# Attention beside moe 1: exponentials go by a transfer into tiles of float32r words and are transposed from there

## The chip, the cores and the metric
The kernel runs on one core of one Trainium2 chip. The metric is the device time of one execution in microseconds (us). TensorE does the matmuls, VectorE, ScalarE and GpSimd the elementwise work (DVE, ACT and POOL in the profile), and 16 DMA engines move data, issued by SyncE (SP), GpSimd or ScalarE.

## The reference
Three steps follow each other, all in float32:

```
attention  q, k, v of 4 x 12 heads x 448 x 64:  q and k normed by rms over 64 and scaled by g_q, g_k
           softmax(q k^T / 8) v  -> x of 1792 tokens x 768
moe 1      sigmoid(x w_gate) * (x w_val), then @ w_out      (768 -> 1536 -> 768)
moe 2      8 experts, each token goes to the one with the largest logit:
           relu(x w1[e]) @ w2[e]  (768 -> 1024 -> 768), times its softmax weight and its output gate
```

## The kernel before, in words
Attention works on 24 pairs of heads. A pair has 8 slots; a slot is 112 queries of one head against all 448 keys, so there are 192 slots (`NSLOT`), numbered n. In `attn_slot(n)` stand: the scores of slot n+1 (two float32r matmuls of 448 columns into PSUM tile `s`), `soft_max(n)` (VectorE multiplies by the inverse norms of the keys and takes the row maximum, `e<-s,rb`, L377 and L380; ScalarE takes the exponential in place and its row sum, L381), `transp(n-2)` (four TensorE transposes of 112 x 112 against `ident` into PSUM tile `t`, L410, evicted to `et` by ScalarE at L418, or by VectorE in one slot of eight, L416), and, once in four slots, `av`, the matmuls of the transposed exponentials with v (L431).

Moe 1 is done in two halves of 896 tokens. Its first half is interleaved with the second half of attention: from slot 101 on, the main loop calls moe steps and attention slots in turn by a table of costs (3.4 for an `up`, 1.0 for a `down`), and between slots 96 and 101 the first weights are fetched. Every moe product takes three matmuls, since x and the weights are split into a high and a low float32r word (`xh`, `xl`, `whi`, `wlo`); `up` is at L555, `down` at L578. The weights of the first half come as 64-bit words: SyncE fetches a piece of 384 KB into `w` (L93), ScalarE and VectorE make float32 of it (L99 to L106), which goes to a buffer in DRAM (`wf`) for the second half of moe 1, and ScalarE and GpSimd or VectorE split it (L121, L123). `lead_turn`, `lead_mul` and `lead_put` (L510 to L540) fold the router's weights into w_out. From 60% of the steps on, rows of zeros are written to the gather table `xg` (L814, L815).

The order in each engine's queue is set by a scheduler that goes by its own estimates of cost; each engine then works its queue in order. Buffers come from pools: `lot("e", 4, 4)` gives the exponentials four buffers, and four more until slot 88 (`l[2] = None`), after which the extra pools are closed and those of moe 1 opened at slot 96. Each instruction waits by semaphores for its operands and its buffer. Moe 2 (from about 960 us) gathers tokens by expert into float32r tiles by DMA and transposes these against a float32r identity (`identr`, L940).

Of the kernel before, what the change touches and what calls it, by code (L numbers as in the profile page):

```python
# [8 lines left out]
F32 = mybir.dt.float32  # L9
F32R = mybir.dt.float32r  # L10
# [7 lines left out]
B, H, S, D = 4, 12, 448, 64  # L18
NT, DM, DFF, NE, FF = 1792, 768, 1536, 8, 1024
CH = 112  # L20
# [14 lines left out]
PARTS = 2  # L35
# [9 lines left out]
def attn_moe_moe_kernel(ctx, tc, qk, tokqk, tokv, g, wup, wout, wr, w1, w2, out):  # L45
    nc = tc.nc
# [3 lines left out]
    const = ctx.enter_context(tc.tile_pool(name="const", bufs=1))  # L50
# [8 lines left out]
    wf = dram.tile([3 * NF, 128, WO], F32, name="wf")  # L59

    ident = const.tile([128, 128], F32, name="ident")
    gg = const.tile([128, 1], F32, name="gg")
    tri = const.tile([128, 128], BF16, name="tri")
    ones = const.tile([128, 128], BF16, name="ones")
# [109 lines left out]
    def lot(name, bufs, more, space=None):  # L174
        kw = {} if space is None else dict(space=space)
        lots[name] = [moe1.enter_context(tc.tile_pool(name=name, bufs=bufs, **kw)), bufs, None, more, {}, kw]
# [6 lines left out]
    def tile_of(name, shape, dtype, tag):  # L183
        pool, bufs, pool2, more, turns, _ = lots[name]
        i = turns.get(tag, 0)
        turns[tag] = i + 1
        if pool2 is not None and i % (bufs + more) >= bufs:
            pool = pool2
        return pool.tile(shape, dtype, tag=tag, name=tag)
# [6 lines left out]
    lot("sw", 1, 0)  # L196
    lot("rs", 1, 1)
    lot("rb", 2, 1)
    lot("e", 4, 4)
    lot("sm", 6, 6)  # L200
    lot("et", 4, 4)
    lot("xr", 1, 2)
# [5 lines left out]
    mp = {}  # L208

    def open_moe():  # L210
        for name, bufs in (("acc", 1), ("h", 3), ("t", 2), ("w64", PARTS), ("wt", 1)):
            mp[name] = moe1.enter_context(tc.tile_pool(name=name, bufs=bufs))
        mp["m"] = moe1.enter_context(tc.tile_pool(name="ps_m", bufs=3, space=PSUM))
        mp["acc_t"] = mp["acc"].tile([128, NBLK, WO], F32, name="acc")
# [82 lines left out]
    def row_bank():  # L297

        if lots["ps_k"][2] is not None:
            return lots["ps_k"][2].tile([128, 4, CH], F32, tag="k", name="k")  # L300
        return tile_of("ps_t", [128, 4, CH], F32, "t")
# [47 lines left out]

    order = [(0, 0), (0, 1), (1, 0), (1, 1), (0, 2), (0, 3), (1, 2), (1, 3)]  # L350
    NSLOT = 8 * NPAIR
    s_t, e_t, et_t, av_t, rs_t = {}, {}, {}, {}, {}
    sum_t = [const.tile([CH, 8, 2], F32, name=f"sum{i}") for i in range(3)]
    for t in sum_t:
# [2 lines left out]
    def scores(n):  # L357
        if not 0 <= n < NSLOT:
            return
        p = n // 8  # L360
        h, c = order[n % 8]
        ps = tile_of("ps_s", [CH, S], F32, "s")
        lhs = Q_t[p][:, h, c * CH:(c + 1) * CH]
        nc.tensor.matmul(ps, lhsT=lhs, rhs=K1_t[p][:, h, :], start=True, stop=False)  # L364
        nc.tensor.matmul(ps, lhsT=lhs, rhs=K2_t[p][:, h, :], start=False, stop=True)  # L365
        s_t[n] = ps

    def soft_max(n):
        if not 0 <= n < NSLOT:
            return  # L370
        p = n // 8
        h, c = order[n % 8]
        ps = s_t.pop(n)
        e = tile_of("e", [128, S], F32, "e")[0:CH]
        m = tile_of("sm", [CH, 2], F32, "m")
        i = h * 4 + c
        nc.vector.tensor_tensor_reduce(  # L377
            out=e, in0=ps, in1=rb_t[p][:, h, :], scale=r_t[p][:, i:i + 1], scalar=-3.0e38, op0=ALU.mult, op1=ALU.max,
            accum_out=m[:, 0:1])
        nc.vector.tensor_reduce(out=m[:, 1:2], in_=m[:, 0:1], axis=AX.X, op=ALU.max, negate=True)  # L380
        nc.scalar.activation(  # L381
            out=e, in_=e, func=ACTF.Exp, scale=1.0, bias=m[:, 1:2], accum_out=sum_t[p % 3][:, i, 0:1])
        e_t[n] = e

    def sums(p):
        sm = tile_of("sm", [CH, 8], F32, "sum")

        nc.vector.tensor_reduce(out=sm, in_=sum_t[p % 3], axis=AX.X, op=ALU.add)
        nc.vector.reciprocal(out=sm, in_=sm)
        ps = row_bank()  # L390
        nc.tensor.transpose(ps[0:8, 0, :], sm, ident[0:CH, 0:CH])
        rr = tile_of("rs", [8, CH], F32, "rr")
        nc.vector.tensor_copy(out=rr, in_=ps[0:8, 0, :])
        nc.sync.dma_start(out=rsd[p], in_=rr)
        t = tile_of("rs", [128, S], F32, "rs")
        for h in range(2):
            nc.sync.dma_start(
                out=t[64 * h:64 * h + 64],
                in_=rsd[p:p + 1, 4 * h:4 * h + 4].rearrange("o c q -> o (c q)").to_broadcast([64, S]))
        rs_t[p] = t  # L400

    def transp(n):
        if not 0 <= n < NSLOT:
            return
        p = n // 8
        h, c = order[n % 8]
        e = e_t.pop(n)
        ps = tile_of("ps_t", [128, 4, CH], F32, "t")
        for kc in range(4):
            nc.tensor.transpose(ps[0:CH, kc, :], e[:, kc * CH:(kc + 1) * CH], ident[0:CH, 0:CH])  # L410
        if c % 2 == 0:
            et_t[p, h, c // 2] = tile_of("et", [CH, 4, 2 * CH], F32, "et")
        et = et_t[p, h, c // 2]
        dst = et[:, :, (c % 2) * CH:(c % 2 + 1) * CH]
        if n % 8 == 2:
            nc.vector.tensor_copy(out=dst, in_=ps[0:CH])  # L416
        else:
            nc.scalar.activation(out=dst, in_=ps[0:CH], func=ACTF.Copy)  # L418

    def av(n):  # L420
        if not 0 <= n < NSLOT or n % 4 != 3:
            return
        p = n // 8
        hf = (n % 8) // 4
        if hf == 0:
            av_t[p] = tile_of("ps_a", [128, S], F32, "a")
        ps = av_t[p]
        ets = [et_t.pop((p, h, hf)) for h in range(2)]
        for kc in range(4):
            for h in range(2):  # L430
                nc.tensor.matmul(  # L431
                    ps[64 * h:64 * h + 64, hf * 2 * CH:(hf + 1) * 2 * CH], lhsT=v_t[p][:, h, kc, :],
                    rhs=ets[h][:, kc, :], start=(kc == 0), stop=(kc == 3))

    def features(p):
        b, pr = divmod(p, H // 2)
        t = tile_of("xr", [128, S], F32, "xr")
        nc.vector.tensor_tensor(out=t, in0=av_t.pop(p), in1=rs_t.pop(p), op=ALU.mult)
        if b < 2:
            hi = x_p.tile([128, S], F32R, tag=f"xh{b}_{pr}", name="xh")  # L440
            lo = x_p.tile([128, S], F32R, tag=f"xl{b}_{pr}", name="xl")
            nc.gpsimd.tensor_copy(out=hi, in_=t)
            nc.gpsimd.tensor_tensor(out=lo, in0=t, in1=hi, op=ALU.subtract)
            xh[b, pr], xl[b, pr] = hi, lo
        else:
            nc.sync.dma_start(out=xs[b - 2, pr], in_=t)
# [33 lines left out]
    def attn_slot(n):  # L480
        p, i = divmod(n, 8)
        scores(n + 1)
        soft_max(n)
        transp(n - 2)
        if i == 0 and n > 0:
            sums(p - 1)
        av(n - 3)
        if i == 4 and n > 8:
            features(p - 1)
        la = 2 if p < NPAIR // 2 - 3 else 1  # L490
        if p == 0:
            prep(i)
        if p > 0 and i == 0:
            splits(p + la)
        if p > 0 and i == 1:
            stats(min(2 * p + 4, p + 6))
            krows(p + la)
        if i == 4:
            load_v(p + 1)
# [272 lines left out]

    def setup():
        make_identity(nc, ident)
        warm = const.tile([128, 1], F32, name="warm")
        nc.vector.memset(warm, 0.0)
        nc.scalar.activation(out=warm, in_=warm, func=ACTF.Exp)
        gt = const.tile([128, 2], F32, name="gt")
        nc.sync.dma_start(out=gt, in_=g)
        attn_loads0()  # L780
        nc.vector.tensor_tensor(out=gg, in0=gt[:, 0:1], in1=gt[:, 1:2], op=ALU.mult)
        nc.vector.tensor_scalar(out=gg, in0=gg, scalar1=float(D) ** -0.5, scalar2=None, op0=ALU.mult)
# [52 lines left out]
    n = 0  # L835
# [4 lines left out]
    n = 1  # L840
    while n < NSLOT // 2 + 5:
        attn_slot(n)
        n += 1
        if n == NSLOT // 2 - 8:
            for l in lots.values():
# [24 lines left out]

    for tg in range(2):
        for k in range(KD):
            t = tile_of("e", [128, S], F32, "e")
            nc.sync.dma_start(out=t, in_=xs[tg, k])
            hi = x_p.tile([128, S], F32R, tag=f"xh{tg}_{k}", name="xh")
            lo = x_p.tile([128, S], F32R, tag=f"xl{tg}_{k}", name="xl")
            nc.scalar.activation(out=hi, in_=t, func=ACTF.Copy)
            (nc.gpsimd if k >= 3 else nc.vector).tensor_tensor(out=lo, in0=t, in1=hi, op=ALU.subtract)
            xh[tg, k], xl[tg, k] = hi, lo
# [308 lines left out]
```

## Time and profile before

| | |
|---|---|
| median of 3 runs | 1289.23 us (1287.64 to 1289.48) |
| profiled execution | 1288.62 us, span of its instructions 1286.8 us |
| TensorE busy | 1185.8 us, 92% of the span, mean granted clock 0.966 |
| VectorE, ScalarE, GpSimd busy | 722.1, 577.1, 382.4 us |
| moved by DMA | 191.92 MB, 149 GB/s on average |

The page gives the span in 40 slices of 32 us; attention alone fills the first six, attention beside moe 1 the next fourteen, the rest of moe 1 goes to about slice 30, and moe 2 is the end. A matmul's duration is from its start to a modelled end, and matmuls are pipelined: what one costs in a stream is the distance to the next one's start. "Idle" before an instruction is the time its engine stood, and the arrow names what released it.

### The profile page before, as it was taken

Reading aid. Unit: us, or ns where it says so; the run is one execution under the profiler, and the core shown is the slowest. Engines: PE = TensorE matmul, PEld = TensorE weight load, DVE = VectorE, ACT = ScalarE, POOL = GpSimd, SP = SyncE. Lnnn points to the kernel's source line nnn. Section 1 sums busy time; section 2 is a strip of 40 time slices with the busy share of each in tenths; the row PEclk is TensorE's granted clock in tenths of the full one; section 3 lists DMA queues with packets and bytes.
Section 4 is the critical chain, followed back from the end, with each engine's and each line's share of the span. In section 5 each row is a group of like instructions: output and inputs, shape, how many; then the busy total and the mean of one; then the engine's idle time right before and its main releaser. Section 6 shows DMA issues by size and latency. Waiting matters only on the chain.

```text
span 1286.8 us, 19940 instructions
## 1 busy us (share of the span) xinstructions
PE 1185.8 (92%) x7089; PEld 1039.4 (81%) x7089; DVE 722.1 (56%) x1709; ACT 577.1 (45%) x1174; POOL 382.4 (30%) x318
## 2 busy tenths in 40 slices
PE   5888888999999898997989999999969999999996
PEld 3665657677778787786879999999959998999996
DVE  7877878877568585775754224433454323333342
ACT  4656755556455353543441331122114434555553
POOL 3555645413132031310232000000023434545453
PEclk9888889899999999998999999999998999999999
DMA  9476666656536279476444121121037355566671
GB/s 219 128 181 172 153 163 201 186 144 184 146 96 196 88 199 234 132 197 151 150 139 136 50 63 50 42 71 50 13 123 273 114 194 186 190 207 222 209 269 43
DMA packets 77054, 191.92 MB, mean 149 GB/s; under 512 B 10617, under 2 KB 27513, under 8 KB 76944
## 3 DMA queue, kind: packets, MB, share of 16 engines
q1 hardware_dynamic: 74496, 179.52, 47.8%
q0 software_dynamic: 2448, 11.03, 2.3%
q8 instruction: 58, 0.95, 0.3%
q14 instruction: 52, 0.43, 0.1%
HBM read 154.43 MB, written 36.81 MB: 149 GB/s over the span
## 4 chain that ended last, share of the span: by engine, by line
PE 50%; DMA 2%; DVE 1%; issue 1%; SPq 0%; POOL 0%; ACT 0%; POOLq 0%; DVEq 0%
PE m L555 16%; PE d L1006 10%; PE m L578 9%; PE u L961 7%; PE d L961 3%; PE d L990 2%; DMA w<-in_wup_dram 1%; PE a L431 1%; PE u L940 1%; DMA raw<-in_w_dram 0%; DMA xg<-acc,slot 0%; PE t L410 0%; DMA g<-xg 0%; PE d L998 0%; PE m L597 0%
## 5 line engine op out<-in xcount | busy, mean ns | idle before, releaser
L121 ACT ACTIVATE whi<-raw 128x768 fp32r<-128x768 f32 (+1 forms) x200 | 167.1, 846 | 283.0 <-PE m L555 57.7
L123 POOL TENSOR_TENSOR wlo<-raw,whi 128x768 fp32r<-128x768 f32 (+1 forms) x100 | 188.9, 1896 | 311.4 <-ACT whi L121 268.4
L555 PE MATMUL m<-xh,whi 128*128 128x448 f32 x576 | 215.1, 374 | 4.5 <-DVE tanh L567 3.1
L555 PE MATMUL m<-xl,whi 128*128 128x448 f32 x576 | 212.4, 369 | 0.0
L555 PE MATMUL m<-xh,wlo 128*128 128x448 f32 x576 | 211.1, 367 | 0.0
L123 DVE TENSOR_TENSOR wlo<-raw,whi 128x768 fp32r<-128x768 f32 (+1 forms) x100 | 99.9, 1003 | 187.8 <-ACT whi L121 187.1
L381 ACT ACTIVATE e<-e,m 112x448 f32<-112x448 f32 x192 | 127.4, 665 | 89.8 <-DVE m L380 80.8
L377 DVE CUSTOM_DVE_ANT_0 e<-s,rb,sy 112x448 f32<-112x448 f32 x192 | 127.5, 672 | 32.2 <-PE s L365 17.6
L555 PEld LDWEIGHTS m<-xh,whi 128*128 128x128 f32 x576 | 109.6, 190 | 16.4 <-DVE tanh L567 3.3
L578 PE MATMUL m<-whi,hhi 128*128 128x392 f32 (+1 forms) x336 | 116.7, 352 | 4.5 <-DVE acc L584 2.7
L364 PE MATMUL s<-K,Q 128*112 128x448 f32 x192 | 87.1, 453 | 34.7 <-DVE m L377 24.5
L410 PE MATMUL t<-ident,e 112*112 112x112 f32 x768 | 109.9, 271 | 9.3 <-ACT et L418 6.4
L555 PEld LDWEIGHTS m<-xl,whi 128*128 128x128 f32 x576 | 109.4, 190 | 9.6 <-issue 1.7
L578 PE MATMUL m<-wlo,hhi 128*128 128x392 f32 (+1 forms) x336 | 115.4, 343 | 1.4 <-POOL wlo L123 1.4
L431 PE MATMUL a<-et,v 112*64 112x224 f32 x768 | 109.5, 379 | 7.7 <-ACT et L418 3.8
L410 PEld LDWEIGHTS t<-ident,e 112*112 112x112 f32 x768 | 87.6, 139 | 35.5 <-ACT et L418 8.8
L555 PEld LDWEIGHTS m<-xh,wlo 128*128 128x128 f32 x576 | 109.0, 189 | 8.6
L578 PE MATMUL m<-whi,hlo 128*128 128x392 f32 (+1 forms) x336 | 114.7, 341 | 0.0
L334 POOL TENSOR_TENSOR Q<-qk,Q 64x896 fp32r<-64x896 f32 (+1 forms) x25 | 56.0, 2240 | 172.4 <-DVE Q L333 93.5
L418 ACT ACTIVATE et<-t 112x448 f32<-112x448 f32 x168 | 87.1, 536 | 28.6 <-PE t L410 28.3
L584 DVE TENSOR_TENSOR acc<-m,acc 128x392 f32<-128x392 f32 (+1 forms) x140 | 77.2, 557 | 33.3 <-PE m L578 32.0
L733 POOL DMA_INDIRECT xg<-acc,slot x14 | 14.4, 1028 | 271.0 <-DVE slot L710 267.4
(209 smaller groups left out, 2399.2 us busy)
## 6 DMA issues: line engine op xcount, KB each, us to landing
raw<-in_w_dram SPq DMA_DIRECT2D x128, 384.0 KB
qk<-in_qk_dram SPq DMA_DIRECT2D x46, 448.0 KB
w<-in_wup_dram SPq DMA_DIRECT2D x48, 384.0 KB
tok<-in_tokqk_dram SPq DMA_DIRECT2D x23, 448.0 KB
wf<-raw SPq DMA_DIRECT2D x24, 384.0 KB
w<-in_wout_dram SPq DMA_DIRECT2D x24, 384.0 KB
raw<-wf SPq DMA_DIRECT2D x24, 384.0 KB
rb<-rkd SPq DMA_DIRECT2D x21, 392.0 KB
```

The costliest lines, as they stand in the source:

```text
L121: nc.scalar.activation(out=hi[:, c:], in_=t[:, c:], func=ACTF.Copy)
L123: eng.tensor_tensor(out=lo[:, c:], in0=t[:, c:], in1=hi[:, c:], op=ALU.subtract)
L364: nc.tensor.matmul(ps, lhsT=lhs, rhs=K1_t[p][:, h, :], start=True, stop=False)
L377: nc.vector.tensor_tensor_reduce(out=e, in0=ps, in1=rb_t[p][:, h, :], scale=r_t[p][:, i:i + 1], scalar=-3.0e38, op0=ALU.mult, op1=ALU.max, ...
L381: nc.scalar.activation(out=e, in_=e, func=ACTF.Exp, scale=1.0, bias=m[:, 1:2], accum_out=sum_t[p % 3][:, i, 0:1])
L410: nc.tensor.transpose(ps[0:CH, kc, :], e[:, kc * CH:(kc + 1) * CH], ident[0:CH, 0:CH])
L418: nc.scalar.activation(out=dst, in_=ps[0:CH], func=ACTF.Copy)
L431: nc.tensor.matmul(ps[64 * h:64 * h + 64, hf * 2 * CH:(hf + 1) * 2 * CH], lhsT=v_t[p][:, h, kc, :], rhs=ets[h][:, kc, :], start=(kc == 0), ...
L555: nc.tensor.matmul(ps[:, 0:S], lhsT=a, rhs=x, start=(n == 0), stop=(n == 3 * KD - 1))
L578: nc.tensor.matmul(ps[:, 0:c1 - c0], lhsT=l, rhs=r, start=(i == 0), stop=(i == 5))
L961: nc.tensor.matmul(ps[:, 0:c], lhsT=a, rhs=x[:, k, 0:c], start=(n == 0), stop=(n == 3 * KD - 1))
L1006: nc.tensor.matmul(ps[i, n][0:rows, 0:384], lhsT=l, rhs=s[:, c0:c0 + 384], start=(f == 0 and q == 0), stop=(f == NF2 - 1 and q == 2))
```

## The change
From slot 96 (`MOVED`) on, ScalarE issues, after the exponential of slot n, a DMA that copies `e` (112 x 448 float32) into a tile `er` of the same size whose words are declared float32r; the bits stay the same. The four transposes of the slot then read `er` and use a float32r identity, `identr1`, made at the start. `er` has two buffers, opened with the pools of moe 1. `e` has two buffers instead of four, and six instead of four more in the first half. At the end of attention, where the features of batches 2 and 3 are read back (`xs`), every second tile is taken from `er`.

```diff
+    identr = const.tile([128, 128], F32R, name="identr1")
-    lot("e", 4, 4)
+    lot("e", 2, 6)
-        for name, bufs in (("acc", 1), ("h", 3), ("t", 2), ("w64", PARTS), ("wt", 1)):
+        for name, bufs in (("acc", 1), ("h", 3), ("t", 2), ("w64", PARTS), ("wt", 1), ("er", 2)):
+    MOVED = NSLOT // 2
+    def move(n):
+
+        if MOVED <= n < NSLOT:
+            er = mp["er"].tile([CH, S], F32R, tag="er", name="er")
+            nc.scalar.dma_start(out=er.bitcast(F32), in_=e_t[n])
+            e_t[n] = er
         for kc in range(4):
-            nc.tensor.transpose(ps[0:CH, kc, :], e[:, kc * CH:(kc + 1) * CH], ident[0:CH, 0:CH])
+            a = e[:, kc * CH:(kc + 1) * CH]
+            if n >= MOVED:
+                nc.tensor.transpose(ps[0:CH, kc, :].bitcast(F32R), a, identr[0:CH, 0:CH])
+            else:
+                nc.tensor.transpose(ps[0:CH, kc, :], a, ident[0:CH, 0:CH])
         transp(n - 2)
+        move(n)
+        nc.vector.tensor_copy(out=identr, in_=ident)
-            t = tile_of("e", [128, S], F32, "e")
+            t = tile_of("e", [128, S], F32, "e") if k % 2 else (
+                mp["er"].tile([128, S], F32R, tag="er", name="er").bitcast(F32))
```

The scheduler lays the queues anew from slot 88 on. ScalarE's queue beside the first `lead_turn` (its eviction is `thi<-m`, L513), before; `e,sum` are the exponentials, `et<-t` the evictions of transposes, `tanh` and `hhi` belong to `up`:

```order
L513 ACTIVATE thi<-m 128x512
L568 ACTIVATE hhi<-tanh 128x448
L418 ACTIVATE et<-t 112x4x112
L381 ACTIVATE e,sum_172<-e,m 112x448
L559 ACTIVATE tanh<-m 128x448
L381 ACTIVATE e,sum_172<-e,m 112x448
L344 ACTIVATE K_3232<-qk,gg 128x896
L418 ACTIVATE et<-t 112x4x112 x2
L381 ACTIVATE e,sum_172<-e,m 112x448
L513 ACTIVATE thi<-m 128x512
```

The same place after the change, where the line numbers are higher (`thi` is L527, `e,sum` L383, `et` L431, the new issue L391):

```order
L527 ACTIVATE thi<-m 128x512
L582 ACTIVATE hhi<-tanh 128x448
L383 ACTIVATE e,sum_173<-e,m 112x448
L431 ACTIVATE et<-t 112x4x112
L391 DMA er<-e 112x448
L383 ACTIVATE e,sum_173<-e,m 112x448
L573 ACTIVATE tanh<-m 128x448
L431 ACTIVATE et<-t 112x4x112
L391 DMA er<-e 112x448
L431 ACTIVATE et<-t 112x4x112
L391 DMA er<-e 112x448
L527 ACTIVATE thi<-m 128x512
```

Each issue stands behind an eviction; the eviction is that of slot n-2, the issue that of slot n.

TensorE's queue where slots 96 to 100 are transposed, before (`s` are scores, `t<-ident,e` the transposes of a slot in fours, `a` the matmuls with v):

```order
L410 MATMUL t<-ident,e 112x112 x4
L431 MATMUL a<-et,v 64x224 x5
L364 MATMUL s<-K_2312,Q 112x448
L365 MATMUL s<-K_2313,Q 112x448
L410 MATMUL t<-ident,e 112x112 x8
L364 MATMUL s<-K_2312,Q 112x448
L365 MATMUL s<-K_2313,Q 112x448
L410 MATMUL t<-ident,e 112x112 x8
```

And after, slots 96 to 99 (`t<-identr_72,er` the transposes from `er`, L569 the `up` matmuls):

```order
L421 MATMUL t<-identr_72,er 112x112 x8
L366 MATMUL s<-K_2314,Q 112x448
L367 MATMUL s<-K_2315,Q 112x448
L366 MATMUL s<-K_2314,Q 112x448
L367 MATMUL s<-K_2315,Q 112x448
L444 MATMUL a<-et,v 64x224
L569 MATMUL m<-xh,whi 128x448 x2
L569 MATMUL m<-xl,whi 128x448
L569 MATMUL m<-xh,wlo 128x448
L569 MATMUL m<-xl,whi 128x448
L569 MATMUL m<-xh,wlo 128x448
L421 MATMUL t<-identr_72,er 112x112 x8
```

Two slots' transposes stand together here, and the scores of two slots and some `up` matmuls between these and the next two.

## Rows read from the trace of the kernel before
**Rows 1.** Page, the span in 40 slices, tenths: TensorE's busy share and granted clock
```profile
PE   5888888999999898997989999999969999999996
PEclk9888889899999999998999999999998999999999
```
**Rows 2.** Window 229 to 640 us, per engine; then groups: busy, mean ns | idle
```profile
229.00:640.00 411.00, 385.33 (x2218) 319.94 (x2217) 289.88 (x714) 205.72 (x447) 95.45 (x68) 0.97 0.58 162
...
L410 PE MATMUL t<-ident,e 112*112 112x112 f32 x384 | 54.2, 262 | 4.8 <-ACT et L418 4.1 <-DVE rk L322 0.8
L418 ACT ACTIVATE et<-t 112x448 f32<-112x448 f32 x84 | 44.5, 536 | 18.7 <-PE t L410 18.5
```
**Rows 3.** Waits of TensorE, 229 to 640 us: total us, times, longest
```profile
PE s L364 <- DVE m L377: 5.5, 2, 3.4
PE m L522 <- DVE tlo L514: 4.2, 2, 3.3
...
PE m L555 <- ACT tanh L559: 0.5, 1, 0.5
```
**Rows 4.** Waits of ScalarE, 229 to 640 us
```profile
ACT raw L99 <- DMA w<-in_wout_dram: 39.2, 15, 6.3
ACT raw L99 <- DMA w<-in_wup_dram: 32.9, 20, 6.0
```
**Rows 5.** Timeline near 506 us: start, us, engine, line [idle before <- releaser]
```profile
506.27 0.56 ACT L99 ACTIVATE raw<-w 128x384 f32<-128x384 f32 x1 [5.97 <-DMA w<-in_wup_dram]
...
508.32 0.60 PE L410 MATMUL t<-ident,e 112*112 112x112 f32 x4 [1.66 <-ACT et L418]
```
**Rows 6.** Timeline of TensorE around four transposes of e
```profile
433.18 0.37 PE L365 MATMUL s<-K,Q 128*112 128x448 f32 x1
433.39 0.55 PE L410 MATMUL t<-ident,e 112*112 112x112 f32 x4
433.71 0.35 PE L522 MATMUL m<-thi,wrs 128*32 128x256 f32 x1
433.90 0.28 PE L522 MATMUL m<-tlo,wrs 128*32 128x256 f32 x1
434.01 0.28 PE L522 MATMUL m<-thi,wrs 128*32 128x256 f32 x1
```
**Rows 7.** L940: min/median/max ns; timeline of TensorE around two of them
```profile
L940 PE MATMUL u<-identr,g x96: 211/225/283, 998.2 to 1246.2; 128*128 128x128 f32 x60, 64*128 64x64 f32 x18, 32*128 32x32 f32 x6, 112*128 112x112 f32 x6
...
1093.11 0.29 PE L940 MATMUL u<-identr,g 128*128 128x128 f32 x2
1093.24 0.41 PE L1006 MATMUL d<-wlo,hh 128*128 128x384 f32 x1
1093.48 0.33 PE L1006 MATMUL d<-whi,hl 128*128 128x384 f32 x1
1093.65 0.34 PE L1006 MATMUL d<-whi,hh 128*128 128x384 f32 x1
```
**Rows 8.** Timeline of TensorE, a block of 128 rows and one of 64
```profile
1241.31 0.40 PE L940 MATMUL u<-identr,g 128*128 128x128 f32 x2
1241.63 0.44 PE L990 MATMUL d<-wlo,hh 128*128 128x384 f32 x1
```
**Rows 9.** Timeline: issue of 384 KB of w, and VectorE's use of it
```profile
384.43 0.34 SPq L93 DMA_DIRECT2D w<-in_wup_dram  x1
...
387.66 0.36 DVE L101 TENSOR_SCALAR w<-w 128x384 int32<-128x384 int32 x1 [0.63 <-DMA w<-in_wup_dram]
```
**Rows 10.** Timeline: issue of 224 KB of xs, and ScalarE's use of it
```profile
666.26 0.32 SPq L874 DMA_DIRECT2D e<-xs  x1
...
670.27 0.58 ACT L877 ACTIVATE xh<-e 128x448 fp32r<-128x448 f32 x1 [1.79 <-DMA e<-xs]
```
**Rows 11.** Chain that ended last, 560 to 600 us: start, us, what
```profile
579.09 5.30 DMA w<-in_wup_dram
...
587.10 5.69 DMA w<-in_wup_dram
```

## What I predict
> **What bounds the kernel now.** I read the page's 40 slices first, then one window over the stretch that the change touches, then the waits of TensorE and ScalarE there, then single places. The slices show TensorE at 8 to 9 tenths nearly everywhere [rows 1]. The 384 transposes of slots 96 to 191, the only ones that change, all start between 229 and 640 us [rows 2]: 411 us for 96 slots, 4.28 us a slot. In that stretch TensorE is busy 385 of 411 us, ScalarE 206, and the DMA engines 0.58 of the time [rows 2]. TensorE's waits there come to 25 us, in eleven rows, of which rows 3 show the first two and the last. So TensorE sets the pace for some 94% of the stretch, and what is taken from its stream should mostly come off the span. The rest is set by the conversion of w_up and w_out on ScalarE and VectorE: ScalarE stands 39.2 + 32.9 us at L99 for the words to land [rows 4], and where one such wait lasted 5.97 us, a transpose stood 1.66 us behind the eviction that was queued after it [rows 5].
>
> **What TensorE gains.** A slot has four float32 transposes of 112 columns. They start 0.10 us apart: (0.55 - 0.26) / 3, with 0.26 the mean of one [rows 2, 6]. 112 columns at 2.4 GHz are 0.047 us, so a float32 column takes two cycles. The next group starts 0.32 us after the first transpose, and its first matmul then holds 0.19 us where the later ones hold 0.12 (433.71, 433.90, 434.01) [rows 6]: 0.32 + 0.07 = 0.39 us a slot. For float32r the trace has the turns of the gathered rows in moe 2. Two of 128 columns start (0.29 - 0.225) = 0.065 us apart, mean of one from the line's own rows; the next group starts 0.13 us after the first, and its first matmul holds 0.24 us where the others hold 0.17 [rows 7]. For four of 112 columns, three steps of 0.065 x 112/128 = 0.057, then 0.06 to the next start and 0.07 of hold: 0.30 us. 0.39 - 0.30 = 0.09 to 0.10 us a slot; I take 0.098, so 96 x 0.098 = **9.4 us**. Where two slots' transposes stand together, as twice in the order shown ahead, the hold is paid once and a slot saves up to 4 x (0.097 - 0.055) = 0.17 us: 16 us if all stood so, which they don't. From below: a pair of a full block and a block of 64 rows in moe 2 takes 0.32 us to the next start [rows 8], no faster than four float32 ones. The new transposes all have 112 rows, so I keep that bound for a rival only.
>
> The Trainium skill speaks against the gain: "TensorE: Matmul & The Clock Gate", section on LDWEIGHTS, has a weight load at its columns over 1.2 GHz, here 93 ns for 112 columns, whatever the data, and in a transpose the data are the weights. By it the loads would keep the pace at 0.093 us where it is 0.097 now, and the gain would be an estimated 96 x 4 x 0.004 = 1.5 us. The trace does not agree: the pairs of moe 2 load 128 columns each and start 0.065 us apart [rows 7].
>
> **What is added.** Per slot, one transfer of 112 x 1792 B = 0.2 MB from e to er, issued by ScalarE. Five costs follow.
>
> ScalarE issues 96 more. SyncE's issue of w took 0.34 us [rows 9]; 0.3 to 0.7 each bounds it, so 29 to 67 us on an engine idle for 205 of 411 us [rows 2]. What hides it is that idle time. What stands behind the issue is in the order: an exponential, a tanh or the eviction of the next slot. Cost 0 to 2 us on the span; I take 0.5.
>
> The new wait. er has two buffers, so transfer n waits for transpose n-2, and transpose n for the transfer to land. In the new ScalarE order the issue stands right behind the eviction of n-2, which waits for the same transpose, so the issue is hardly ever held by more than was waited for anyway. Between the end of transpose n-2 and the start of transpose n must fit the eviction, 0.54 us [rows 2], some 0.15 of hand-over, and issue to landing, L. L for this transfer no trace row shows. Below: 384 KB issued at 384.43 was used by a waiting VectorE at 387.66, 3.2 us [rows 9]; half the size could be nearer 2.5. The nearest in size is 224 KB of xs, 4.0 us from 666.26 to a waiting ScalarE at 670.27, the last of a run of such loads [rows 10]. Above: 5.3 and 5.7 us for w in the crowded part near 580 us [rows 11]. ScalarE's queue holds nothing else, so I take the 3.2, and the need is 3.9 us. The Trainium skill ("DMA: Bandwidth & Descriptors", section "Issuing engines are not separate DMA queues") has all issues run on the same 16 engines and interleave, so that an own queue would save only the place in line; no run here shows it yet, and by it I should take the 4.0 of rows 10 and the 8.7 below. I walked the new TensorE order with the steps of rows 6 (0.20 us for a matmul of 448 columns, in proportion for others): the work between transposes n-2 and n is 6.4 us at the median over 94 slots, 2.5 at the least, under 3.9 in 4 slots and under 5 in 11. The shortfalls add to 3.7 us at L = 3.2, 8.7 at L = 4, 14 at 4.5 and 32 at 5.3; at 2.5 they are under 2. The walk lacks the waits and half-clock parts (the stretch lasts 411 us, the walked work about 350), which lengthen the distances, so I take **3 us**.
>
> DMA load. 96 x 0.2 = 19.3 MB more. The engines moved 162 GB/s at a share of 0.58 [rows 2], so 279 GB/s when busy, and 19.3 MB are 69 us, or 0.17 of the stretch: 0.58 becomes 0.75. Late w words cost: ScalarE's 72 us of waits at L99 [rows 4] would grow by some 10 to 20%, 7 to 14 us, and of such waits TensorE felt a part (25 us of its own against ScalarE's 72 at L99 alone) [rows 3, 4]. I take **2 us**, bounds 0 and 8.
>
> Fewer buffers of e. From slot 88 there are two instead of four until er opens at slot 96, so the write of e for n waits for transpose n-2: while the new order leaves some 4 us of matmuls between one pair of slots and the next. From slot 96 on two of e and two of er are four again. 0 to 2 us, taken at 0.
>
> The cast of identr1 and its place, and every second xs reload going into er: one VectorE instruction before the first tokens land, and as many buffers as before. 0.
>
> The sum: -9.4 + 0.5 + 3 + 2 + 0 = **-3.9 us**. The profiled execution took 1288.62 us (span 1286.8 and 1.8 around it), so 1284.7 by its measure; the median of the runs is 1289.23, 0.6 above it, so I predict **1285.3 us**.
>
> **Rivals.**
> Landing takes TensorE's place (slower). One mechanism: the loop transpose n-2, eviction, issue, landing, transpose n closes over two slots, and TensorE, in order, stands at the transpose with all moe matmuls behind it. It decides from where the shortfalls pass what is left of the gain, 9.4 - 2.5 = 6.9 us, an L of about 3.8 us. At L = 4.5 (between 3.9 and 5.3, in rows 10 and 11) it is -9.4 + 2.5 + 14 = +7, **1296 us**; with 5.3 throughout it would be +25. For it: the window's DMA share rises to 0.75, and two of the three landings in rows 9 to 11 are above the point. Against it: they shared one queue with others, and the median distance is 6.4 us.
>
> The gain is taken back elsewhere (same). TensorE gets ahead by 9 us, and meets the w words: ScalarE's long waits at L99, up to 6.3 us each [rows 4], come at the time that DMA and VectorE set, not TensorE. With half of the 9.4 lost so, -4.7 + 5.5 = about +1, **1290 us**. For it: the crowded parts near 505 and 580 us. Against it: only a few of the waits in rows 3 are longer than 1.5 us.
>
> The change does not shorten the transposes (slower or same): the loads bind, or each pays what the blocks of 64 rows pay. As it is with the block of 64 rows [rows 8], the gain is 0 and the costs 5.5 stay: **1295 us**. Against it rows 7, and that all four have the same 112 rows. (By the Trainium skill's weight load, named above, it would be 1293.)
>
> **How the numbers follow.** Forecast 0.46, landing 0.24, taken back 0.23, no shortening 0.07. What a measurement of this kernel can tell from no change is about 0.2%, 2.6 us. The forecast's own range is 1279 (a gain of 12 us, landing under 3 us) to 1288, of which about a tenth lies within 0.2%; of no shortening most lies above. Faster 0.44, same 0.27, slower 0.29. The range for 8 in 10 reaches from 1278 to 1298, with the landing case up to an L just above 4.5; longer landings are left out.
>
> **What would show it.** In the new profile the four transposes of a slot should start about 0.057 us apart at full clock, and the 384 of them take clearly less TensorE time than the 54 us of rows 2. TensorE's waits by releaser should name the transfer er with 2 to 5 us in all; over 10 us there, with landings of 4 us and more, proves the landing rival. Waits at L99's successor well above 72 us with TensorE's waits on tanh, tlo and et grown show the DMA load. Steps of 0.09 us or more between the transposes would prove the third. A stretch before slot 96 that is longer would show a cost of the two buffers that I put at nothing.

## The result, and the profile after

The changed kernel takes 1305.7 us (median of 5 runs) against 1289.23 us: **1.39% slower**, ratio 1.0139, 95% interval 1.011 to 1.0168. The profiled execution took 1308.13 us, its span 1306.2. The forecast was 1285.3, faster.

Where the time went was read from the first part of the program, up to the first `up` of the second half of moe 1, which starts at 700.6 us before and at 717.1 after. So 16.5 of the 19.4 us of longer span arise up to there; the other 2.9 were not followed. The window of that part, before, then after (length; busy time of PE, PEld, DVE, ACT, POOL; granted clock, DMA share, GB/s):

```profile
0.00:700.60 700.60, 622.54 (x3636) 502.44 (x3637) 504.91 (x1295) 360.31 (x801) 236.23 (x228) 0.95 0.60 165
```
```profile
0.00:717.10 717.10, 623.95 (x3635) 494.98 (x3636) 487.71 (x1296) 360.75 (x801) 231.42 (x228) 0.95 0.67 188
```

TensorE does the same number of matmuls, within one, in the same busy time, within 1.4 us, at the same clock. It stands idle 93.2 us where it stood 78.1. So 15.1 of the 16.5 us are time in which TensorE waits; that its cheaper transposes don't show in the busy time is taken up below.

The waits of the changed kernel over 195 to 665 us (total us, times, longest), VectorE's first:

```profile
DVE e L379 <- DMA er<-e: 57.5, 28, 5.4
DVE e L379 <- ACT et L431: 1.5, 1, 1.5
...
PE t L421 <- DMA er<-e: 17.7, 20, 2.2
PE s L366 <- DVE m L379: 13.1, 17, 2.4
```

The row of TensorE's transposes is new, and I had looked for it: 17.7 us for the landing [rows 3 have none]. VectorE's row I had not looked for: VectorE stands 57.5 us before it may write scores into a buffer of `e` (L379), because the transfer still reads it. The kernel before has, in the same window, this:

```profile
DVE e L377 <- PE s L365: 12.6, 9, 3.1
DVE e L377 <- PE t L410: 0.7, 2, 0.4
```

There the write of `e` waits for its input, the scores, and nearly never for its buffer. After, it waits for the buffer. How it runs stands in the chain that ended last, changed kernel, 600 to 640 us (start, us, what):

```profile
622.25 4.79 DMA er<-e
...
627.17 0.68 DVE e L379
...
628.56 0.76 ACT e L383 x2
...
629.35 2.54 DMA er<-e
...
631.92 0.68 DVE e L379
...
635.19 4.59 DMA er<-e
```

This is a loop: transfer, write of the next scores into the freed buffer, exponential, next transfer. Over 500 to 640 us the largest items of the chain in the kernel before were TensorE's `down` and `up`, 10.0% and 8.6% of that stretch; after, the largest is `er<-e`, 12.4%. What VectorE holds back is not only `e`. It works in order, and the bias step of ScalarE's exponential, the conversions of `w` and the evictions stand behind. ScalarE's wait for the row maxima of VectorE, over 229 to 660 us, is

```profile
ACT e L383 <- DVE m L382: 92.3, 55, 6.7
ACT raw L100 <- DMA w<-in_wout_dram: 36.9, 17, 4.3
ACT raw L100 <- DMA w<-in_wup_dram: 24.3, 16, 3.0
```

where the first of them was 54.2 before, over 229 to 640 us. The waits for `w` did not grow: 61.2 us against 72.1 [rows 4], although the share of the DMA engines over 229 to 640 us rose to 0.69 from 0.58 [rows 2].

The chain, however, reaches back only to 561 us, and the loss is older than that. The next windows are cut where TensorE has taken up the same work in both kernels, counted in columns of its matmuls without the transposes of `e`: at 225 us before and 225.3 after, then at 300 and 316.7. Before, then after:

```profile
225.00:300.00 75.00, 71.45 (x410) 55.41 (x410) 59.42 (x149) 43.52 (x96) 27.77 (x25) 0.95 0.56 160
300.00:700.60 400.60, 373.47 (x2133) 316.59 (x2130) 267.67 (x639) 181.43 (x385) 89.24 (x60) 0.97 0.56 160
```
```profile
225.30:316.70 91.40, 76.11 (x407) 57.27 (x406) 55.50 (x145) 43.80 (x96) 26.07 (x26) 0.89 0.60 176
316.70:717.10 400.40, 369.41 (x2141) 308.40 (x2140) 258.11 (x648) 183.55 (x390) 87.95 (x59) 0.98 0.68 197
```

The first stretch takes 91.4 us where it took 75.0, and that is the whole loss. TensorE's idle time there grows from 3.6 to 15.3 us, and its busy time from 71.5 to 76.1 at a granted clock of 0.89 instead of 0.95. Over 240 to 260 us the clock is 0.62, so for most of that time at the lower of its two levels (1.2 GHz); before that TensorE had stood for 0.80, 1.97 and 1.05 us between 226 and 236. The rest takes 400.4 us against 400.6. In it lie 39.7 of VectorE's 57.5 us of waits for `er<-e` and 12.4 of TensorE's 17.7, and they cost no time on balance: TensorE's idle time is 3.9 us longer there and its busy time 4.1 us shorter. So the sum of a wait is not its price. The second timing of the changed kernel, reported below, loses its time in the same place: the same work takes from 224.1 to 316.8 us there, at a clock of 0.89.

The transposes did become shorter. The group of their line after (min/median/max ns, first and last start), which answers to L410 in [rows 2]:

```profile
L421 PE MATMUL t<-identr,er x384: 214/240/442, 235.8 to 660.8; 112*112 112x112 f32 x192
```

They begin some 7 us later than before and take 425 us of the program instead of 411. Timeline of TensorE after, at three places (answers to [rows 6]):

```profile
477.53 0.81 PE L421 MATMUL t<-identr,er 112*112 112x112 f32 x8
478.17 0.42 PE L592 MATMUL m<-whi,hhi 128*128 128x392 f32 x1
...
641.19 0.43 PE L421 MATMUL t<-identr,er 112*112 112x112 f32 x4
641.45 0.43 PE L366 MATMUL s<-K,Q 128*112 128x448 f32 x1
641.72 0.37 PE L367 MATMUL s<-K,Q 128*112 128x448 f32 x1
...
660.63 0.43 PE L421 MATMUL t<-identr,er 112*112 112x112 f32 x4
660.90 0.63 PE L524 MATMUL m<-ident,raw 128*128 128x128 f32 x4
```

Four float32r transposes start (0.43 - 0.24) / 3 = 0.063 us apart on average, with 0.24 the median of one; eight start (0.81 - 0.24) / 7 = 0.081 apart. A short run is quick and a long one is not. The next matmul follows 0.26 us after the first transpose, and holds 0.27 (641.45 to 641.72) where matmuls of this size take 0.20. So a slot takes 0.26 + 0.07 = 0.33 us, where it took 0.39 before.

Landing can be read where a waiting engine picks the transfer up (timeline after: the two issues on ScalarE, then TensorE):

```profile
239.57 0.54 ACTq L391 DMA_DIRECT2D er<-e  x1
...
240.98 0.52 ACTq L391 DMA_DIRECT2D er<-e  x1
...
245.73 1.15 PE L421 MATMUL t<-identr,er 112*112 112x112 f32 x8 [1.14 <-DMA er<-e]
```

From the second issue it is 4.75 us. The four transfers that the chain holds between 195 and 660 us last 2.54 to 5.51 us.

### The profile page after: what moved, and what is told of

It is laid out like the page before. It is cut to its first block, busy times and chain, and to the rows that moved or that the text cites. A ratio compares the mean times of both kernels' runs of the same rounds, so it can differ in the third digit from the quotient of the medians.

```text
span 1306.2 us, 20236 instructions
## 1 busy us (share of the span) xinstructions
PE 1188.0 (91%) x7089; PEld 1032.7 (79%) x7089; DVE 705.7 (54%) x1710; ACT 577.4 (44%) x1174; POOL 377.4 (29%) x318
## 4 chain that ended last, share of the span: by engine, by line
PE 46%; DMA 6%; DVE 2%; SPq 1%; issue 1%; ACT 0%; POOL 0%; POOLq 0%; DVEq 0%; ACTq 0%
PE m L569 15%; PE d L1022 9%; PE m L592 8%; PE u L977 7%; PE d L977 3%; PE d L1006 2%; DMA er<-e 1%; DMA w<-in_wout_dram 1%; DMA w<-in_wup_dram 1%; DMA xg<-zrow 1%; PE u L956 1%; DMA raw<-in_w_dram 0%; SPq L920 0%; DMA g<-xg 0%; PE d L1014 0%
## 5 line engine op out<-in xcount | busy, mean ns | idle before, releaser
L569 PE MATMUL m<-xh,whi 128*128 128x448 f32 x576 | 216.8, 377 | 0.8 <-POOL xh L455 0.3
L569 PE MATMUL m<-xl,whi 128*128 128x448 f32 x576 | 213.9, 371 | 0.1
L569 PE MATMUL m<-xh,wlo 128*128 128x448 f32 x576 | 212.4, 369 | 0.0
L383 ACT ACTIVATE e<-e,m 112x448 f32<-112x448 f32 x192 | 127.4, 664 | 131.5 <-DVE m L382 121.3
L379 DVE CUSTOM_DVE_ANT_0 e<-s,rb,sy 112x448 f32<-112x448 f32 x192 | 127.8, 674 | 83.8 <-DMA er<-e 57.5
L569 PEld LDWEIGHTS m<-xh,whi 128*128 128x128 f32 x576 | 110.1, 191 | 12.8 <-issue 2.0
L569 PEld LDWEIGHTS m<-xl,whi 128*128 128x128 f32 x576 | 110.3, 191 | 9.4 <-POOL xl L456 0.7
L569 PEld LDWEIGHTS m<-xh,wlo 128*128 128x128 f32 x576 | 109.9, 191 | 9.1 <-issue 0.3
L335 POOL TENSOR_TENSOR Q<-qk,Q 64x896 fp32r<-64x896 f32 (+1 forms) x25 | 52.8, 2110 | 206.1 <-DVE Q L334 141.8
L431 ACT ACTIVATE et<-t 112x448 f32<-112x448 f32 x168 | 86.5, 533 | 30.2 <-PE t L421 18.0
L444 PEld LDWEIGHTS a<-et,v 112*64 112x64 f32 x768 | 59.6, 143 | 40.6 <-issue 11.8
L366 PEld LDWEIGHTS s<-K,Q 128*112 128x112 f32 x192 | 36.8, 192 | 58.5 <-DVE m L379 39.8
```

The costliest lines, as they stand in the source:

```text
L379: nc.vector.tensor_tensor_reduce(out=e, in0=ps, in1=rb_t[p][:, h, :], scale=r_t[p][:, i:i + 1], scalar=-3.0e38, op0=ALU.mult, op1=ALU.max, ...
L383: nc.scalar.activation(out=e, in_=e, func=ACTF.Exp, scale=1.0, bias=m[:, 1:2], accum_out=sum_t[p % 3][:, i, 0:1])
L444: nc.tensor.matmul(ps[64 * h:64 * h + 64, hf * 2 * CH:(hf + 1) * 2 * CH], lhsT=v_t[p][:, h, kc, :], rhs=ets[h][:, kc, :], start=(kc == 0), ...
L569: nc.tensor.matmul(ps[:, 0:S], lhsT=a, rhs=x, start=(n == 0), stop=(n == 3 * KD - 1))
```

## The experiments

The question was which of four suspects costs the time: the buffers of `e` that are held (A), TensorE's wait for the landing (B), the load on the DMA engines (C), or ScalarE's issues (D). All ratios are to the kernel before, timed on the same chip; "before" differed between chips (1280.57 to 1289.35 us), so times of different groups are not compared. Each kernel is laid out anew by the scheduler, so a control differs from its partner by more than its edit. How much that can be, two kernels without a transfer and with float32 transposes show: 1.0024 and 1.0101, 0.8% apart, on different chips, for no cause that I found.

The expectations, written before, use other letters: theory L is the landing (A or B here, as each says), theory D the load (C here), theory B the smaller number of buffers of `e`. Times in them count from the 1289.23 us of the kernel before.

**No transfer.** ScalarE's exponential writes straight into `er` (it rounds to float32r words, which the reference doesn't); nothing else changes.

```diff
+        x = mp["er"].tile([CH, S], F32R, tag="er", name="er") if n >= MOVED else e
-            out=e, in_=e, func=ACTF.Exp, ...
-        e_t[n] = e
+            out=x, in_=e, func=ACTF.Exp, ...
+        e_t[n] = x
```

> From slot 96 on the exponential is written straight into er as float32r words (rounded by ScalarE), and no transfer is issued; buffers (two of e, two of er) and the float32r transposes stay as in the changed kernel. The exponentials are thus coarser than the reference's. Theory L (the landing of the transfer, on which the transposes and the next write of e wait, costs the time): the gain of the transposes alone is left, 1283 to 1288 us. Theory D (the 19.3 MB of extra DMA traffic make the weights late): the same, since the traffic is gone. Theory B (two buffers of e instead of four, above all from slot 88 to 96, cost it): it stays at 1296 us or above.

Measured: 1269.84 us, ratio 0.9906 (0.9876 to 0.9936), the only kernel here that is faster than before, and by more than any theory gave (0.1 to 0.5%). Its waits, 195 to 665 us, and its transposes:

```profile
DVE e L379 <- PE s L367: 6.8, 6, 2.9
DVE e L379 <- ACT er L384: 4.3, 8, 1.0
```
```profile
L422 PE MATMUL t<-identr,er 112*112 112x112 f32 x384 | 43.8, 235 | 2.4 <-ACT et L432 2.1 <-ACT er L384 0.3
```

With two buffers of `e` and two of `er`, as in the changed kernel, the wait for a buffer is 4.3 us: the buffer comes free at the end of the exponential. The number of buffers is not what costs, but when they come free. The loss lies in the transfer.

**The transfer, its result unused.** The transposes stay float32 and read `e`; nobody waits for the data.

```diff
-            e_t[n] = er
-            if n >= MOVED:
+            if False:
```

> The 96 transfers are issued as in the changed kernel, but nothing reads er: the transposes read e in float32 as before. The write of a later slot into e still waits for the landing; the transposes do not. Theory L, if the wait of TensorE's transposes for the landing is what counts: 1290 to 1296 us. Theory L, if VectorE's wait for a free e is what counts: 1300 us or more. Theory D: 1298 us or more whatever waits, with longer waits of ScalarE and VectorE for w_up and w_out. Theory B alone: 1300 us.

Measured: ratio 1.0193 (1.0148 to 1.0239). TensorE doesn't wait for landings here (B is out of this kernel), and yet the whole loss is there. The waits, 195 to 665 us:

```profile
DVE e L379 <- DMA er<-e: 40.4, 20, 4.4
DVE e L379 <- PE t L422: 6.4, 10, 2.4
...
PE s L366 <- DVE m L379: 19.4, 16, 2.9
```

**The same with four buffers of `e`** (paid with one of `et`).

```diff
-    lot("e", 2, 6)
+    lot("e", 4, 4)
-    lot("et", 4, 4)
+    lot("et", 3, 5)
```

> The unused transfers with float32 transposes, but four buffers of e (three of et). If VectorE's wait for e is the larger part of what the transfers cost: 0.7 to 1.1% above before, where two buffers gave 1.93%. If the load is: 1.4% or more.

Measured: ratio 1.0024 (1.0004 to 1.0044). All 96 full transfers are still issued and still move their 19.3 MB, and the loss is 0.24% instead of 1.93%, less than either case expected. The waits of this kernel:

```profile
DVE e L379 <- PE s L367: 9.3, 11, 2.7
...
DVE e L379 <- DMA er<-e: 2.5, 2, 1.7
...
PE s L366 <- DVE m L379: 4.6, 5, 2.0
```

This pair shows A, and shows that C and D together are small: 40.4 us of VectorE's wait become 2.5, and 1.7% of the time (some 21 us) goes with them.

**Two buffers without a transfer.**

```diff
-        if MOVED <= n < NSLOT:
+        if False:
```

(and float32 transposes from `e`, as above)

> No transfer and float32 transposes from e as before, but two buffers of e from slot 88 on (er is opened and not used in attention). Theory B: 1297 us or more, with the loss already there at slot 96, where the changed kernel is 7 us late. Theories L and D: within 4 us of the kernel before, 1287 to 1293 us.

Measured: ratio 1.0024 (1.0 to 1.0047). Two buffers that wait for a read cost 21.4 us of VectorE's time, and little of the end (the second line is the first transpose of slot 96):

```profile
DVE e L379 <- PE t L423: 21.4, 19, 3.7
...
235.52 0.66 PE L423 MATMUL t<-ident,e 112*112 112x112 f32 x3
```

Slot 96 comes late here too, at 235.5 us, as in the changed kernel (235.8; 228.8 before), with no transfer in the program; here that is made up by the end. Set beside the unused transfers with the same buffers (1.0193), this is a second pair that puts 1.7% on the transfers.

**The changed kernel with four buffers of `e`** (and three of `et`, as above).

> The changed kernel with four buffers of e instead of two from slot 88 on; the room comes from et, which has three instead of four. Transfers and float32r transposes as in the changed kernel, er with two buffers. Theory L by VectorE's write of e (57.5 us of waits for er there in the changed kernel's profile): that wait all but goes and the time falls to 1288 to 1296 us. Theory L by the loop over er's two buffers (transpose n-2, transfer n, transpose n): TensorE's 17.7 us of waits stay, and the time stays at 1300 us or more. Theory D: 1300 us or more. Theory B: as low as the first.

Measured: ratio 1.0096 (1.0056 to 1.0135). The waits:

```profile
DVE e L379 <- DMA er<-e: 11.6, 12, 2.2
DVE e L379 <- PE s L367: 8.5, 7, 4.3
...
PE t L421 <- DMA er<-e: 16.7, 9, 5.4
```

A falls from 57.5 to 11.6 us and part of the time comes back; B stays, 16.7 us. Its interval touches that of the changed kernel (1.011 to 1.0168), so how much of the time comes back is uncertain. It lies clear of the kernel with four buffers and unused transfers (1.0004 to 1.0044), which differs from it only in what is transposed: 0.72% slower, about 9 us, although its transposes are 5 us faster. That would put B at about 14 us, almost three times the gain. But 0.72% is no more than the 0.8% that kernels without a transfer lie apart, so this price is argued and not shown. The chain doesn't price it either: over 500 to 640 us `er<-e` is its largest item here too, with 13.4%, more than in the slower changed kernel.

**The changed kernel again, and with four buffers of `er`** (and three of `et`). The second asks whether the loop that I had priced, over two buffers of `er`, is the one that holds.

> The changed kernel once more, on the same chip as the three others, so that they can be set against it: 1.1 to 1.7% above before.

> The changed kernel with four buffers of er instead of two (room from et, three instead of four), e with two. The loop transpose n-2, transfer n, transpose n of the prediction is opened; a write of e still waits for a landing. If that loop is what holds: 0.6% above before or less. If the write of e holds (theory L by VectorE): about as the changed kernel, 1.2 to 1.6% above before. Theory D: as the changed kernel too.

```diff
-        for name, bufs in (..., ("wt", 1), ("er", 2)):
+        for name, bufs in (..., ("wt", 1), ("er", 4)):
```

Measured: 1.0179 (1.0128 to 1.0231), and 1.0245 (1.0172 to 1.0318) with four: no better, the intervals overlap. VectorE's and TensorE's waits for the transfer are 46.0 and 18.0 us in the one, 50.6 and 18.9 in the other. So more buffers of `er` bring nothing back that these runs can see (the kernel pays with a buffer of `et`, which cost 0.4% elsewhere).

**Smaller transfers, and transfers that nobody waits for.** First 8 of the 448 columns, result unused, two buffers of `e`; then full transfers from two tiles of zeros, paced by one GpSimd copy per slot, and the same with 8 columns. The last two leave `e` and `er` out of the matter: only load and issues remain. `et` has three buffers in them.

```diff
-            nc.scalar.dma_start(out=er.bitcast(F32), in_=e_t[n])
+            nc.scalar.dma_start(out=er.bitcast(F32)[:, 0:8], in_=e_t[n][:, 0:8])
```

> As the kernel with unused transfers (float32 transposes of e, two buffers of e), but each transfer carries 8 of the 448 columns. The write of e still waits for a landing, about 2 us after the issue, and ScalarE still issues 96 times; the load of 19.3 MB is gone. Theory D (the load costs): within 5 us of the kernel with the same buffers and no transfer, 0 to 0.6% above before. Theory L by the wait for e (a landing of any size holds VectorE): most of the 21 us by which the unused transfers lost against no transfer stay, 1.2% above before or more.

> The load without the waits: after each exponential of slots 96 to 191 ScalarE issues a transfer of the full 196 KB from one of two tiles of zeros (GpSimd copies a column of row sums into it first, which paces the transfers), nothing reads the target, and no buffer of e hangs on the landing. Float32 transposes of e, two buffers of e, three of et. Theory D: 1.0% above before or more. Theory L: 0 to 0.6% above before.

> The load-only kernel with transfers of 8 of 448 columns: 96 issues on ScalarE at the same places, no load, no buffer of e that hangs on a landing; float32 transposes, two buffers of e, three of et. If ScalarE's time for the issue (about 0.5 us each, 50 us in all) is what costs: 0.8% above before or more, as the load-only kernel. If the load costs: 0 to 0.5%.

```diff
-            nc.scalar.dma_start(out=er.bitcast(F32), in_=e_t[n])
+            nc.gpsimd.tensor_copy(out=t[:, 0:1], in_=sum_t[n // 8 % 3][:, h * 4 + c, 0:1])
+            nc.scalar.dma_start(out=er.bitcast(F32), in_=t)
```

Measured: 1.0102 (1.0069 to 1.0136) with 8 columns, and VectorE's wait for the transfer 15.6 us instead of 40.4; load and issues 1.0108 (1.0052 to 1.0164); issues alone 1.007 (1.0045 to 1.0095). The first lies between its two expectations and separates nothing by itself, since fewer bytes land sooner too: in the traces a transfer takes 2.3 us at the median from its issue to the end of its last packet, where the full one takes 3.4. Load and issues reach what theory D asked for, and the issues alone lie between the bands; but most of both is not the transfers', as the control below shows. The last two were on different chips, and were run again beside each other, with a control for the three buffers of `et` on the chip of the first issue kernel:

> Control for the kernels that took room from et: no transfer, float32 transposes, two buffers of e, and three of et instead of four. If et's fourth buffer does not matter: 0 to 0.5% above before, as with four of et; if it does, 0.7% or more, and the loads measured with three of et are smaller by as much.

> The load-only kernel once more, beside the issues alone. Theory D: 0.4% or more above the kernel with the issues alone. Theory L: within 0.2% of it.

> The issues alone once more: 0.6 to 0.8% above before, of which most is et's third buffer.

Measured: the control (two buffers of `e`, three of `et`, no transfer) 1.0062 (1.0042 to 1.0083), so the issues add 0.08% there, within the intervals. Load and issues 1.0114 (1.0087 to 1.0142), issues alone 1.0091 (1.0064 to 1.0119): C is 0.2%, again within the intervals (and just above theory L's bound; the issues alone came out above the 0.6 to 0.8% expected). D and C are each too small for these runs to tell from nothing. My conclusion on A doesn't need them.

**SyncE issues the transfers**, in the changed kernel.

```diff
-            nc.scalar.dma_start(out=er.bitcast(F32), in_=e_t[n])
+            nc.sync.dma_start(out=er.bitcast(F32), in_=e_t[n])
```

> The changed kernel with SyncE issuing the 96 transfers, in its queue among the weights and other loads. If ScalarE's time for the issue counts: 1.2% above before or less. If the landing counts (it now stands in line behind other transfers, and SyncE in order behind its waits): 1.8% above before or more.

Measured: 1.0178 (1.0142 to 1.0214), as with ScalarE's and just short of what the second case asked for. TensorE waits longer for the transfer:

```profile
DVE e L379 <- DMA er<-e: 59.4, 36, 4.5
...
PE t L421 <- DMA er<-e: 28.8, 20, 3.7
```

So ScalarE's own queue gained no time that these runs can see, though its waits were shorter. The rule of the Trainium skill that I had weighed ("DMA: Bandwidth & Descriptors", section "Issuing engines are not separate DMA queues") now has a run here whose time agrees with it, 1.0178 against 1.0139 and 1.0179; the waits, 28.8 us against 17.7 and 18.0, differ.

**What makes the version without a transfer fast.** The same separate tiles, but float32 words and float32 transposes; and the rounded version for all 192 slots.

```diff
+        x = mp["er"].tile([CH, S], F32, tag="er", name="er") if n >= MOVED else e
```

> The version without a transfer, but the exponential goes into er as float32 words and the transposes are float32. Same buffers (two of e, free after the exponential, and two of er). If the float32r transposes are the whole of that version's gain: 0 to 0.3% from before. If their gain is what the steps in the traces give (0.052 us in a slot, 5 us in all) and the rest is the buffers: 0.4 to 0.6% below before.

```diff
-    MOVED = NSLOT // 2
+    MOVED = 0
```

> The version without a transfer (ScalarE writes the exponential as float32r words into er) for all 192 slots instead of the last 96. If TensorE's stream bounds the first half of attention too: 1.3 to 2% below before; if that half is bound by its loads and by VectorE, 0.7 to 1.2% below, as with half of the slots.

Measured: 1.0101 (1.0073 to 1.0129), and 1.0026 (1.0005 to 1.0047). Both lie outside every case expected. The transposes of the first:

```profile
L424 PE MATMUL t<-ident,er 112*112 112x112 f32 x384 | 54.5, 261 | 1.9 <-DVE rk L323 1.4 <-ACT et L432 0.4
```

Between it and the rounded one (43.8 us above) lie 1.95% of the time, some 25 us, where the steps of the transposes give 5. And in all slots, with the buffers shared out differently (`e` 2 and 2, `er` 2 and 3), the rounding gains nothing. So the steps of the transposes alone don't explain it. That the order that the scheduler lays is another part I take to be likely; no run here shows it, and what gains the rest is open. The version without a transfer, from slot 96 on, remains the best kernel of this study, if its rounding is accepted.

## Why the prediction was wrong

The step that failed is the last of my costs: "Fewer buffers of e ... From slot 96 on two of e and two of er are four again. 0 to 2 us, taken at 0." I counted buffers and not what releases them. Before, a buffer of `e` was held until its transposes had read it. After, it is held until the transfer has landed, and `er` doesn't help, since scores are written to `e` alone. I did write that `e` has two from slot 88 and that its write waits, but put the end of it at slot 96. My own sign of that cost came, slot 96 is 7 us late; but two buffers without a transfer are as late there and make it up. The lasting part begins at slot 96: from there to 316.7 us the changed kernel falls behind and stays so. The pair of kernels with unused transfers prices it: 1.0193 with two buffers, 1.0024 with four, some 21 us. In the changed kernel itself, four buffers bring it from 1.0139 and 1.0179 (two timings) to 1.0096, some 5 to 11 us, with intervals that touch.

- **The gain of 9.4 us** was mis-sized. I took the step of pairs, 0.065 us for 128 columns [rows 7], for a run of four. Measured, a slot goes from 0.39 to 0.33 or 0.34 us: 0.052 x 96 = 5.0 us. A pair is too short to show the pace of a run: in a run of four the first two steps do take 0.057 us at the median, but the third 0.078, and eight in a row start 0.081 apart on average. So I was too quick with the Trainium skill's weight load ("TensorE: Matmul & The Clock Gate", section on LDWEIGHTS): the estimate of 93 ns from it is longer than the paces seen here, but nearer to the 81 ns of a run of eight than my 57; the 63 of a run of four, as most slots have, are nearer to mine. The gain of 5.0 us lies between my 9.4 and the 1.5 estimated from that page.
- **The new wait of 3 us** was mis-sized: TensorE waits 17.7 us, for a price that may be about 14 (0.72% between 1.0096 and 1.0024, and the 5 us that the transposes gave; not shown, as said there). I took a landing of 3.2 us. In the changed kernel's trace the 96 transfers take 2.1 to 7.6 us from issue to the end of the last packet, 3.5 at the median, and 15 of them over 5: the size was near, the spread was missing. Where the chain holds them they last 2.54 to 5.51, and the one above 4.75. The distances that I walked (median 6.4 us between transposes n-2 and n) were those of TensorE's stream. Issue n, I take it, came later than I had it, because VectorE wrote `e` late, so less of the distance was left for the landing. The loop that I closed over `er` isn't the one that holds: four buffers of `er` bring nothing back.
- **ScalarE's issues, 0.5 us, and the load, 2 us**: not refuted. The controls give 0.08% and 0.2%, both within their intervals; the waits for `w` didn't grow, against what I expected. The DMA share of the stretch rose to 0.69, where I had 0.75, as the stretch also became longer.
- **The rivals.** The landing case had the sign and one of the places (TensorE stands at the transpose for `er`), with 1296 us. It named the wrong loop and missed VectorE. (Of the four landings in rows 9 to 11 three lie above its point of 3.8 us, not two of three.) The granted clock, which fell to 0.62 where TensorE stood most, was in no case. "No shortening" is refuted by the steps, and "taken back elsewhere" by the waits for `w`.

The two prices don't add up freely. Held buffers cost 1.7% where TensorE doesn't wait for landings, and 0.4 to 0.8% where it does, probably since both waits hold up the same chain. That buffers of `e` held by the transfer make the kernel slower is shown, by two pairs of 1.7% and the waits in them. That TensorE waits for the landing is shown too, but not its price. How the 16.5 us of the medians divide between them these runs don't settle, since the scheduler moves other work with every edit.

## What to carry to other kernels

When a copy is put into a chain of engines, ask of every buffer what releases it now. A buffer read by a DMA is held for issue and landing (2.1 to 7.6 us here) and not for the read of an engine, and the price appears at the engine that writes it next, with all that stands behind in its queue. So give the copied buffer, not the copy, the depth. Take the pace of a run of instructions from a run of that length. And look for the place where a kernel falls behind before you add up its waits: most of the waits here cost no time on balance.

## What the runs showed that I had not expected

- Float32r transposes of 112 columns: four start 0.063 us apart on average, eight 0.081, against 0.097 in float32 [rows 6]. Within one run the first steps are the short ones: in fours 0.058, 0.057 and 0.078 us at the median.
- A transfer of 8 of 448 columns, 32 bytes a row, is not as much quicker as it is smaller: 1.4 to 5.4 us from issue to the end of the last packet, 2.3 at the median, where the unused full transfers take 2.2 to 7.8, 3.4 at the median.
- One buffer of `et` fewer moved the time by 0.4% (1.0062 against 1.0024, intervals 1.0042 to 1.0083 and 1.0 to 1.0047, on different chips), more than the 0.2% that the load of 19.3 MB moved it, though neither is clear of the intervals.
